# Raw weights loaded from the loop's second step on, and the first pair's queries loaded once and doubled by GpSimd

## The chip, the core and the metric

One core of a Trainium2 chip runs the whole program. The metric is the device time of one execution in microseconds; three runs of the kernel before have a median of 945.22 us. A core has five engines with queues of their own: TensorE (PE, matrix products and transposes; PEld is its weight load), VectorE (DVE), ScalarE (ACT), GpSimd (POOL) and SyncE (SP), which here only issues transfers. ScalarE and GpSimd can issue transfers too. Sixteen DMA engines move the data.

## What is computed

Attention over 4 batches of 8 heads (576 rows of 64), in which only scores within `tau` of the row's maximum count; then a two-dimensional Fourier transform whose real part is added, a norm, an MLP with two weight matrices, and a gated layer. All in float32.

```python
scores = scale * np.matmul(q, k.transpose(0, 1, 3, 2))
thresh = np.max(scores, axis=-1, keepdims=True) - tau
scores = np.where(scores >= thresh, scores, -1000000000.0)
attn = np.exp(scores - max); attn = attn / (sum + 1e-09); x = attn @ v
...
u = x + np.real(np.fft.fft(np.fft.fft(x, axis=1), axis=2))
un = (u - mu) / np.sqrt(var + 1e-06)
y = u + np.maximum(un @ w_ch1, 0.0) @ w_ch2
...
out = sigmoid(causal_conv(y, conv_w)) * (y @ w_val) @ w_out
```

## The kernel before

The program is written in the order in which each engine is to run it; no scheduler reorders anything. It has three stages: an attention loop that also does the Fourier transform and prepares the MLP's weights (to about 385 us), the MLP, and the gated layer.

**The loop.** Heads are taken in 16 pairs. A pair has nine tiles of 128 rows of scores, and one step `u` of the loop handles two tiles, so a pair lasts four and a half steps. In each step the atoms of the string `ORDER` are written out one after the other: for the step's two tiles the row maxima on VectorE (L571) and the threshold (L574, once in each step), the exponentials on ScalarE (L578), the masked product on VectorE (L588), and the next two tiles' scores on TensorE (L559). The tiles of the step before are normalised on GpSimd (L595), and those of two steps before are transposed on TensorE (L629). Between them `filler` puts matrix work from queues: the preparation of the next pair (`g_prep_qk`), the products with the values, and the Fourier transform.

**A pair's loads.** `load_qk(p, second)` brings the keys (`kn`, two loads of 128 KB, and a small one into `tn`), the last 64 query rows of both heads (`tn`, two small loads of the same rows), and the first 512 query rows (`qn`). Index `j` of `qn` is a copy: each head's queries are loaded twice from memory, for `j` = 0 and 1, so that a transpose gives the queries in both halves of the partitions. The keys go through SyncE's queue; for pair 0 `second` is ScalarE's queue, and for all later pairs it is SyncE's. The pool of these tiles has one buffer, so a pair's loads wait until the transposes of the pair before have read theirs. `g_prep_qk` then transposes on TensorE: keys (L244), last rows (L254), head 0's queries and head 1's (L263), with copies out of PSUM by VectorE (L250, L258) and ScalarE (L257, L265). For pair 0 this stands ahead of the loop, and the first scores need all of it.

**The raw weights.** The MLP's weights arrive as 64-bit words and are split into a high and a low part. They come in pieces of 512 KB; three raw buffers and two conversion rooms exist during the loop. `load_raw` issues a piece's load on GpSimd's queue whenever a raw buffer is free; `tick`, called at the end of each step, advances the clock (`clock[0]`) by one, hands on finished pieces and calls `load_raw`. The first such call is at the end of step 0, with the clock at 1, and it issues three loads. Nothing stands ahead of them on GpSimd's queue that waits for anything. A further call, `hooks["begin"]` at `u == 1`, finds no free buffer. A piece's conversion may begin when the clock is four (`LOAD`) past its load. It is a list of operations (L96 to L106 in `stages`): L96 and L97 on VectorE, L98 and L99 on ScalarE, L100, L101 and L102 on VectorE, and L106 on GpSimd, handed out by the atoms `WD`, `WA` and `WP`, a few in each step; so a piece in the loop visits VectorE in three steps. The first 18 pieces (`EARLY`) go back to memory (`e_h`, `e_l`, L921) and come again later; from the 19th on a piece needs a place that opens only behind the loop. Each piece's raw buffer is loaded anew at the end of the step in which it is finished, so the pieces follow one another at a fixed distance of three steps.

Of the kernel before, what the change touches and what calls it, by code (L numbers as in the profile page):

```python
# [21 lines left out]
B, H, S, D = 4, 8, 576, 64  # L22
# [4 lines left out]
MAIN, TAIL = 512, 64  # L27
# [37 lines left out]
@with_exitstack  # L65
def fused_kernel(ctx: ExitStack, tc: tile.TileContext, a: dict, out: bass.AP):
    dram = ctx.enter_context(tc.tile_pool(name="dram", bufs=1, space=DRAM))
    u_d = [dram.tile([DM, S], F32, name=f"u_d{b}") for b in range(B)]
    y_d = [dram.tile([DM, S], F32, name=f"y_d{b}") for b in range(B)]
    with tc.manual_schedule():  # L70
        wide = Wide(tc, ctx)
        conv_w = ConvW(tc, ctx, a, wide)
        fft = ctx.enter_context(ExitStack())
        with tc.tile_pool(name="ps_f", bufs=2, space=PSUM, side="right") as ps_f:
            hooks = {}
            attention = attention_fft(tc, fft, ps_f, a, u_d, dram, conv_w, hooks)
            mlp(tc, fft, ps_f, attention, hooks, a, u_d, y_d, dram, wide, conv_w.cw, out)
# [57 lines left out]
def attention_fft(tc, right, ps_f, a, u_d, dram, conv_w, hooks):  # L135
    nc = tc.nc
    PE, DVE, ACT, POOL, SP = nc.tensor, nc.vector, nc.scalar, nc.gpsimd, nc.sync
    left, right1 = ExitStack(), ExitStack()
    with ExitStack() as right2, ExitStack() as right2b, ExitStack() as right3, ExitStack() as right4, ExitStack() as scores, ExitStack() as turned:
# [39 lines left out]
        def load_qk(p, second=SP):  # L179
            b, hs = p // NP, slice(2 * (p % NP), 2 * (p % NP) + 2)  # L180
            kn = nat_p.tile([128, 2, 2, 2, D], F32, tag="kn", name="kn")
            qn = nat_p.tile([128, 2, 4, 2, D], F32, tag="qn", name="qn")
            tn = nat_p.tile([96, 2, 2, D], F32, tag="tn", name="tn")
            k, q = a["k"][b, hs].rearrange("h (g p) d -> p h g d", g=2), a["q"][b, hs]
            for j in range(2):
                SP.dma_start(out=kn[:, j], in_=k[j * 128:j * 128 + 128])
            SP.dma_start(out=tn[0:32], in_=k[256:HALF])
            for j in range(2):
                second.dma_start(out=tn[32:96, :, j], in_=q[:, MAIN:S].rearrange("h p d -> p h d"))
            for h in range(2):  # L190
                for j in range(2):
                    second.dma_start(out=qn[:, h, :, j], in_=q[h, 0:MAIN].rearrange("(t p) d -> p t d", p=128))
            nat[p] = tn, kn, qn

        def load_v(p):
# [37 lines left out]
        def g_prep_qk(p):  # L233
# [33 lines left out]
            if 0 < p < NPAIR - 1:  # L267
                load_qk(p + 1)
# [375 lines left out]
        LAG = 4  # L644
        SP.dma_start(out=ident, in_=a["ident"])
        load_qk(0, ACT)
        DVE.tensor_scalar(out=atau, in0=tau, scalar1=-1.0, scalar2=None, op0=ALU.mult)
        DVE.tensor_tensor(out=atau, in0=atau, in1=tau, op=ALU.max)
# [6 lines left out]
        while q_prep:  # L655
            fill(1e9)
            flush()
        load_qk(1)
        emit_s(0)
        emit_s(1)  # L660

        spare = 0.0
# [6 lines left out]
        for u in range(NT // 2 + 3):  # L669
            t = 2 * u  # L670
            on = [x for x in (t, t + 1) if x < NT]
            state["tile"] = t
            for x in on:
                p, h, i = tiles[x]
# [68 lines left out]
            for atom in ORDER.split():  # L743
                env[atom]()
            tq.clear()
            if u == 1:
                hooks["begin"]()
            hooks["tick"]()
            if left and NPAIR - 1 in kq:
                left.close()  # L750
# [33 lines left out]
def mlp(tc, right, ps_f, attention, hooks, a, u_d, y_d, dram, wide, cw, out):  # L784
    nc = tc.nc
    PE, DVE, ACT, POOL, SP = nc.tensor, nc.vector, nc.scalar, nc.gpsimd, nc.sync
    KB, FB = DM // 128, DFF // 128
# [5 lines left out]
    with ExitStack() as ctx, ExitStack() as top, ExitStack() as top2:  # L793
        def pool(name, bufs, stack=ctx, **kw):
            return stack.enter_context(tc.tile_pool(name=name, bufs=bufs, reuse_waits="tile", **kw))
# [3 lines left out]
        pieces = []  # L799
# [8 lines left out]
        heads = [0, 0]  # L808
        raws, spare = {}, {"raw": deque(), "cv": deque()}
        active, outbox, stored = deque(), [], deque()  # L810
        at, loaded, clock = [0], [0], [0]
# [42 lines left out]
        def more_room(kind, name):  # L854
            spare[kind].append((pool(name, 1), kind))
            load_raw()

        def load_raw():

            while spare["raw"] and loaded[0] < (len(pieces) if heads[1] == FB else 2 * FB):  # L860
                k = loaded[0]
                loaded[0] += 1
                src, _ = pieces[k]
                room = spare["raw"].popleft()
                room_pool, tag = room
                raws[k] = room, room_pool.tile([128, 512, 2], I32, tag=tag, name="raw", bufs=1), clock[0]
                d = raws[k][1].rearrange("p n t -> p (n t)")
                POOL.dma_start(out=d if len(src.shape) == 2 else d.rearrange("p (k f) -> p k f", k=KB), in_=src)
# [40 lines left out]
        def tick():  # L909

            clock[0] += 1
            while spent and spent[0][0] <= clock[0]:
                nxt[1] -= 1
                give(spent.popleft()[1])
            while stored and stored[0][0] <= clock[0]:
                spare["cv"].append(stored.popleft()[1])
            for k, room, dst in outbox:
                j, i = pieces[k][1]
                if isinstance(j, str) or k < EARLY:
                    for t, d in zip(dst, e_d[k] if k < EARLY else [d[i * 128:(i + 1) * 128] for d in w_d[j]]):  # L920
                        SP.dma_start(out=d, in_=f32(t))  # L921
                    written.add(k)
                    if k in wanted:
                        place(k)
                else:
                    placed.add(k)
                stored.append((clock[0] + (STORE if tail is None else 0), room))
                spare["raw"].append(raws.pop(k)[0])
            outbox.clear()
            load_raw()  # L930
# [233 lines left out]

        for kind in ("raw", "raw", "raw", "cv", "cv"):
            spare[kind].append((pool(f"mlp_{kind}{len(spare[kind])}", 1), kind))
        hooks["begin"] = load_raw

        norm, centred = None, True

# [362 lines left out]
```

## Time and profile before

| | us |
|---|---|
| median of 3 runs | 945.22 |
| lowest and highest run | 945.05, 945.52 |
| the profiled execution | 940.76 |
| its span | 939.0 |
| TensorE busy in it | 882.5 |
| VectorE busy | 561.6 |
| ScalarE busy | 453.0 |
| GpSimd busy | 365.0 |

The rows come from the one profiled execution, so times are placed on its span of 939.0 us, which starts at 0. A row of the timeline gives start, duration, engine, line, operation, output and input and count; what stands in brackets is the idle time of the engine ahead of it and what ended that. A queue that only issues transfers has a q behind its engine's name (SPq, ACTq). Line numbers are those of the kernel before.

### The profile page before, as it was taken

What the parts mean: (1) busy time and instruction counts of PE and PEld (TensorE: products, weight loads), DVE (VectorE), ACT (ScalarE), POOL (GpSimd) and SP (SyncE); (2) the same over time, 40 slices, a digit from 0 to 9 for tenths busy, and PEclk for the clock granted to TensorE, in tenths of its full rate; (3) what the DMA queues carried; (4) which work ended last, traced back from release to release, by engine and by line L of the source; (5) the groups of instructions that cost most, each with busy time, mean ns of one, the idle gap of its engine ahead of it and who ended that gap; (6) DMA issues with size and microseconds to landing.
All of it is one profiled execution on the core that took longest, in us unless ns stands there. A gap on an engine that the chain in (4) does not pass through costs nothing. (4 is left out here: it accounts for less than half of the span.)

```text
span 939.0 us, 14896 instructions
## 1 busy us (share of the span) xinstructions
PE 882.5 (94%) x5232; PEld 705.2 (75%) x5232; DVE 561.6 (60%) x1240; ACT 453.0 (48%) x915; POOL 365.0 (39%) x449
## 2 busy tenths in 40 slices
PE   3889899999999999899998999999999999999998
PEld 2555576656655675478876999999999989998897
DVE  4888888878887776415597243443412275735750
ACT  3777787777776766526355133213211313214432
POOL 1474654674457536613553421312111011037421
PEclk9999999999999999999998999999999999999999
DMA  7675545566555731496359523212120050233211
GB/s 173 164 191 130 165 115 163 159 195 152 168 149 166 186 96 61 145 351 211 106 194 359 213 90 123 86 45 84 45 73 1 1 170 11 90 129 118 74 46 68
DMA packets 136339, 123.61 MB, mean 132 GB/s; under 512 B 86742, under 2 KB 100294, under 8 KB 136264
## 3 DMA queue, kind: packets, MB, share of 16 engines
q1 hardware_dynamic: 126760, 97.57, 33.9%
q0 software_dynamic: 6960, 24.49, 8.5%
q10 hardware_dynamic: 2544, 0.59, 0.4%
q8 instruction: 42, 0.69, 0.3%
q14 instruction: 33, 0.27, 0.1%
HBM read 90.11 MB, written 37.22 MB: 136 GB/s over the span
## 5 line engine op out<-in xcount | busy, mean ns | idle before, releaser
L1060 DVE SCALAR_TENSOR_TENSOR hl<-h,hh 128x448 fp32r<-128x448 f32 (+1 forms) x80 | 51.0, 637 | 204.1 <-ACT hh L1059 204.1
L1059 ACT ACTIVATE hh<-h 128x448 fp32r<-128x448 f32 (+1 forms) x80 | 44.5, 556 | 256.6 <-PE h L1056 256.6
L595 POOL TENSOR_SCALAR p<-p,su 128x576 f32<-128x576 f32 x144 | 108.8, 762 | 90.3 <-DVE su L685 74.1
L588 DVE SCALAR_TENSOR_TENSOR p<-s,thr,e 128x576 f32<-128x576 f32 x144 | 112.4, 815 | 32.2 <-ACT e L578 14.4
L559 PE MATMUL s<-kt,qt 64*128 64x288 f32 (+1 forms) x640 | 99.6, 441 | 27.1 <-DVE p L588 27.1
L1072 PE MATMUL c<-hl,w1h 128*128 128x448 f32 (+1 forms) x320 | 118.9, 371 | 0.7 <-DVE hl L1060 0.7
L1072 PE MATMUL c<-hh,w1h 128*128 128x448 f32 (+1 forms) x320 | 119.0, 372 | 0.0
L1072 PE MATMUL c<-hh,w1l 128*128 128x448 f32 (+1 forms) x320 | 118.8, 371 | 0.0
L578 ACT ACTIVATE e<-s,neg 128x576 f32<-128x576 f32 x144 | 99.4, 737 | 26.1 <-DVE neg L571 25.8
L571 DVE TENSOR_REDUCE neg<-s 128x1 f32<-128x576 f32 x144 | 101.4, 745 | 14.8 <-PE s L559 14.6
L559 PEld LDWEIGHTS s<-kt,qt 64*128 64x128 f32 (+1 forms) x640 | 45.2, 175 | 69.0 <-issue 27.8
L638 ACT ACTIVATE m<-t 128x512 f32<-128x512 f32 x144 | 84.6, 588 | 6.8 <-PE t L629 6.8
L1056 PE MATMUL h<-unh,w0l 128*128 128x448 f32 (+1 forms) x320 | 81.3, 376 | 3.9 <-POOL w0l L106 3.8
L1056 PE MATMUL h<-unh,w0h 128*128 128x448 f32 (+1 forms) x320 | 81.0, 375 | 3.0 <-ACT w0h L105 2.2
L304 PE MATMUL f<-m,v 128*64 128x320 f32 (+1 forms) x512 | 81.9, 422 | 1.5 <-ACT m L638 1.2
L629 PE MATMUL t<-ident,p 128*128 128x128 f32 x576 | 77.7, 277 | 3.4 <-POOL xf L334 1.9
L1056 PE MATMUL h<-unl,w0h 128*128 128x448 f32 (+1 forms) x320 | 80.7, 374 | 0.0
L629 PEld LDWEIGHTS t<-ident,p 128*128 128x128 f32 x576 | 63.6, 140 | 19.2 <-issue 9.3
L1056 PEld LDWEIGHTS h<-unh,w0l 128*128 128x128 f32 x320 | 60.3, 189 | 12.6 <-POOL w0l L106 5.4
L1056 PEld LDWEIGHTS h<-unh,w0h 128*128 128x128 f32 x320 | 60.1, 189 | 11.4 <-ACT w0h L105 3.0
L106 POOL TENSOR_TENSOR ct<-raw 128x512 fp32r<-128x512 f32 x26 | 28.8, 1113 | 99.5 <-DVE raw L102 55.0
L1072 PEld LDWEIGHTS c<-hl,w1h 128*128 128x128 f32 x320 | 60.1, 188 | 8.0 <-DVE hl L1060 1.1
(218 smaller groups left out, 1575.4 us busy)
## 6 DMA issues: line engine op xcount, KB each, us to landing
raw<-in_moe_w_ch POOLq DMA_DIRECT2D x32, 512.0 KB, 5.5
qn<-in_q SPq DMA_DIRECT2D x60, 128.0 KB, 3.5
xs<-xt SPq DMA_DIRECT2D x16, 288.0 KB, 3.6
e_h<-cx SPq DMA_DIRECT2D x18, 256.0 KB, 3.8
e_l<-ct SPq DMA_DIRECT2D x18, 256.0 KB, 5.8
w0h<-e_h SPq DMA_DIRECT2D x18, 256.0 KB, 16.1
w0l<-e_l SPq DMA_DIRECT2D x18, 256.0 KB
w1h<-e_h SPq DMA_DIRECT2D x18, 256.0 KB, 5.5
```

What stands on the lines that cost most here:

```text
L304: PE.matmul(out=f[h * 64:h * 64 + 64, 0:n], lhsT=w, rhs=r, start=(t == 0), stop=(t == 4))
L559: PE.matmul(out=s[o, c, 0:HALF], lhsT=qt[w, hh, q], rhs=kt[w, hh, :], start=True, stop=True)
L571: DVE.tensor_reduce(out=neg[i][:, j, 0:1], in_=sc[g][:, :, 0:HALF], axis=AX.XY, op=ALU.max, negate=True)
L578: ACT.activation(e, sc[g][:, :, 0:HALF], AF.Exp, bias=neg[g // 2][:, g % 2, 0:1], scale=1.0)
L588: DVE.scalar_tensor_tensor(out=p_view(g).rearrange("p (a b) -> p a b", a=2), in0=sc.pop(g)[:, :, 0:HALF], scalar=thr[g // 2][:, j], in1=ex ...
L595: POOL.tensor_scalar(out=v, in0=v, scalar1=su, scalar2=1.0, op0=ALU.mult, op1=ALU.mult)
L629: PE.matmul(out=f[:, t, :], lhsT=pv[:, t * 128:(t + 1) * 128], rhs=ident, is_transpose=True, start=(t == 0), stop=(t == 3))
L638: tq.append(lambda: ACT.activation(o, fv, AF.Copy))
L1056: PE.matmul(out=f[:, 0:n], lhsT=ww[:, k * 128:(k + 1) * 128], rhs=x[:, k, 0:n], start=(i == 0), stop=(i == 3 * KB - 1))
L1059: ACT.activation(hh, f[:, 0:n], AF.Relu)
L1060: DVE.scalar_tensor_tensor(out=hl, in0=f[:, 0:n], scalar=0.0, in1=f32(hh), op0=ALU.max, op1=ALU.subtract)
L1072: PE.matmul(out=ch[c][o][:, 0:n], lhsT=ww[:, o * 128:(o + 1) * 128], rhs=x, start=(at_ == 0 and i == 0), stop=(at_ == FB - 1 and i == 2))
```

## The change

`load_raw` loads nothing while the clock is 1 or less, so the first three raw loads are issued at the end of step 1 in place of step 0. The call `hooks["begin"]` is gone. For pair 0 alone (the branch in which `second` is not SyncE) each head's queries are loaded once, into `j` = 0, and GpSimd copies them to `j` = 1; the order of ScalarE's loads is now head 0's queries, the two loads of last rows, head 1's queries. For the other pairs the loads stay as they were.

```diff
@@ load_qk
-            for j in range(2):
-                second.dma_start(out=tn[32:96, :, j], in_=q[:, MAIN:S].rearrange("h p d -> p h d"))
-            for h in range(2):
+
+            def queries(h, j):
+                second.dma_start(out=qn[:, h, :, j], in_=q[h, 0:MAIN].rearrange("(t p) d -> p t d", p=128))
+
+            def last_queries():
                 for j in range(2):
-                    second.dma_start(out=qn[:, h, :, j], in_=q[h, 0:MAIN].rearrange("(t p) d -> p t d", p=128))
+                    second.dma_start(out=tn[32:96, :, j], in_=q[:, MAIN:S].rearrange("h p d -> p h d"))
+
+            if second is SP:
+                last_queries()
+                for h in range(2):
+                    for j in range(2):
+                        queries(h, j)
+            else:
+                for h in range(2):
+                    queries(h, 0)
+                    if h == 0:
+                        last_queries()
+                    POOL.tensor_copy(qn[:, h, :, 1], qn[:, h, :, 0])
             nat[p] = tn, kn, qn
@@ attention loop
-            if u == 1:
-                hooks["begin"]()
             hooks["tick"]()
@@ load_raw
-            while spare["raw"] and loaded[0] < (len(pieces) if heads[1] == FB else 2 * FB):
+            while clock[0] > 1 and spare["raw"] and loaded[0] < (len(pieces) if heads[1] == FB else 2 * FB):
@@ mlp
-        hooks["begin"] = load_raw
```

What this moves, at three places. Lines of the changed kernel are other numbers: its L609 is the normalisation L595, its L880 the raw load L868.

GpSimd's queue from the program's start on, before:

```order
L1529 UNCONDITIONAL_BRANCH
L868 DMA raw<-in_moe_w_ch 128x4x256
L868 DMA raw<-in_moe_w_ch 128x1024
L868 DMA raw<-in_moe_w_ch 128x4x256
L595 ISA
L595 TENSOR_SCALAR p<-p,su 128x576 x2
L206 DMA cdh<-in_cdh 128x1032
```

and now (its L206 COPY is the new copy of the queries, its L220 the load of the constants):

```order
L1540 UNCONDITIONAL_BRANCH
L206 COPY qn<-qn 128x4x64 x2
L609 ISA
L609 TENSOR_SCALAR p<-p,su 128x576 x2
L880 DMA raw<-in_moe_w_ch 128x4x256
L880 DMA raw<-in_moe_w_ch 128x1024
L880 DMA raw<-in_moe_w_ch 128x4x256
L220 DMA cdh<-in_cdh 128x1032
```

The three raw loads went from ahead of step 1's two normalisations to behind them, and the two copies stand first.

ScalarE's queue at the start, with the semaphores that a row waits for (`tn` are the last rows, `qn` the queries of one head), before:

```order
L165 DMA tau_sb<-in_tau 128x1
L167 ACT_TABLE_LOAD
L167 ACTIVATE atau<-alpha 128x1 [waits DVE_49]
L189 DMA tn<-in_q 64x2x64 x2
L192 DMA qn<-in_q 128x4x64
L192 DMA qn<-in_q 128x4x64 [waits DMAHW0_49]
L192 DMA qn<-in_q 128x4x64 [waits DMAHW2_49]
L192 DMA qn<-in_q 128x4x64 [waits DMAHW4_49]
```

and now:

```order
L165 DMA tau_sb<-in_tau 128x1
L167 ACT_TABLE_LOAD
L167 ACTIVATE atau<-alpha 128x1 [waits DVE_49]
L190 DMA qn<-in_q 128x4x64
L194 DMA tn<-in_q 64x2x64 x2
L190 DMA qn<-in_q 128x4x64 [waits DMAHW0_49]
```

Two loads are gone, head 0's queries moved ahead of the last rows, and head 1's, the last, wait for the semaphore for which the second query load waited before.

VectorE in two steps of the loop, the first of which has the keys' copies of a new pair (L250 and L258; now L264 and L272), before; L588 are the masked products (now L602), L685 the reciprocal that opens a step (now L699):

```order
L588 SCALAR_TENSOR_TENSOR p,su<-s,thr,e 128x576 x2
L250 COPY kt<-f 128x2x256
L258 COPY kt<-f 128x2x32
L101 SCALAR_TENSOR_TENSOR raw<-raw,ct 128x512
L102 TENSOR_SCALAR raw<-cx 128x512
L96 TENSOR_SCALAR cx<-raw 128x512
L685 RECIPROCAL su<-su 128x2
L571 TENSOR_REDUCE neg_193<-s 128x1 x2
L574 TENSOR_REDUCE thr<-neg_193 128x2
L588 SCALAR_TENSOR_TENSOR p,su<-s,thr,e 128x576 x2
L97 TENSOR_SCALAR ct<-raw 128x512
L685 RECIPROCAL su<-su 128x2
```

and now:

```order
L602 SCALAR_TENSOR_TENSOR p,su<-s,thr,e 128x576 x2
L264 COPY kt<-f 128x2x256
L272 COPY kt<-f 128x2x32
L100 SCALAR_TENSOR_TENSOR cx<-raw,cx 128x512
L699 RECIPROCAL su<-su 128x2
L585 TENSOR_REDUCE neg_193<-s 128x1 x2
L588 TENSOR_REDUCE thr<-neg_193 128x2
L602 SCALAR_TENSOR_TENSOR p,su<-s,thr,e 128x576 x2
L101 SCALAR_TENSOR_TENSOR raw<-raw,ct 128x512
L102 TENSOR_SCALAR raw<-cx 128x512
L96 TENSOR_SCALAR cx<-raw 128x512
L699 RECIPROCAL su<-su 128x2
```

The three operations L101, L102 and L96 moved from the step with the keys' copies into the next. The same shift by one step runs through the whole loop on VectorE, ScalarE and GpSimd (steps with the keys' copies and these three together: five before, none now), and SyncE's stores of the finished pieces move with it. TensorE's order is the same in every row, and behind the loop every engine's order is the same.

## Rows read from the trace of the kernel before

**Rows 1.** Busy time by stretch; columns: stretch, length, busy of each engine, clock, DMA.

```profile
core 0: us, PE busy (x) PEld busy (x) DVE busy (x) ACT busy (x) POOL busy (x), PEclk, DMA share, GB/s
...
512.00:707.00 195.00, 195.00 (x955) 178.83 (x954) 72.10 (x127) 48.70 (x87) 44.50 (x43) 1.00 0.29 100
```

**Rows 2.** Timeline of the first 16 us; start, duration, engine, line, operation.

```profile
1.20 0.96 SPq L186 DMA_DIRECT2D kn<-in_k  x2
1.26 2.26 POOL L868 DMA_DIRECT2D raw<-in_moe_w_ch  x3 [0.81 <-POOLq L1522]
...
10.50 0.90 PE L244 MATMUL f<-ident,kn 128*128 128x128 f32 x3 [5.25 <-DMA kn<-in_k]
...
13.21 0.71 PEld L263 LDWEIGHTS f<-ident,qn 128*128 128x128 f32 x4 [0.23 <-issue]
```

**Rows 3.** Timeline, ScalarE's queue at 3.8 us: the second query load.

```profile
3.87 0.64 ACTq L192 DMA_DIRECT2D qn<-in_q  x1
```

**Rows 4.** Busy time by stretch, as in rows 1.

```profile
6.00:8.00 2.00, 0.00 (x0) 0.00 (x0) 0.00 (x0) 0.00 (x0) 0.00 (x0) 1.00 1.06 350
...
16.00:32.00 16.00, 10.21 (x71) 6.17 (x72) 13.60 (x35) 10.23 (x20) 5.89 (x9) 1.00 0.80 188
```

**Rows 5.** DMA issues of the whole run; count, size of each, median us to landing.

```profile
qn<-in_q SPq DMA_DIRECT2D x60, 128.0 KB, 3.5
...
kn<-in_k SPq DMA_DIRECT2D x32, 128.0 KB, 3.2
```

**Rows 6.** DMA issues from 14 to 23 us: a value load behind queries.

```profile
v<-in_v SPq DMA_DIRECT2D x1, 128.0 KB, 5.4
```

**Rows 7.** Groups on GpSimd by shape: count, busy us, mean ns, idle before.

```profile
L595 POOL TENSOR_SCALAR p<-p,su 128x576 f32<-128x576 f32 x144 | 108.8, 762 | 90.3 <-DVE su L685 74.1 <-PE f L263 10.0 <-PE s L559 4.0
...
L334 POOL COPY xf<-xt 128x2 f32<-128x2 f32 x16 | 3.1, 193 | 1.0
```

**Rows 8.** Timeline of 19 to 29 us, GpSimd and its reader.

```profile
19.73 1.47 POOL L595 TENSOR_SCALAR p<-p,su 128x576 f32<-128x576 f32 x2 [16.22 <-DVE su L685]
...
21.16 0.59 POOL L206 DMA_DIRECT2D cdh<-in_cdh  x1
...
24.39 1.46 POOL L595 TENSOR_SCALAR p<-p,su 128x576 f32<-128x576 f32 x2 [2.64 <-DVE su L685]
...
28.29 0.87 PE L629 MATMUL t<-ident,p 128*128 128x128 f32 x6
```

**Rows 9.** Line 868 from 30 to 385 us; durations in ns, min/median/max.

```profile
L868 POOL DMA_DIRECT2D raw<-in_moe_w_ch x18: 582/728/872, 55.9 to 318.8; - x18
```

**Rows 10.** Groups on VectorE from 20 to 385 us: the conversion's operations.

```profile
L97 DVE TENSOR_SCALAR ct<-raw 128x512 int32<-128x512 int32 x18 | 16.6, 921 | 0.0
L100 DVE SCALAR_TENSOR_TENSOR cx<-raw,cx 128x512 int32<-128x512 int32 x18 | 13.3, 738 | 0.0
L101 DVE SCALAR_TENSOR_TENSOR raw<-raw,ct 128x512 f32<-128x512 uint32 x18 | 13.1, 728 | 0.0
...
L96 DVE TENSOR_SCALAR cx<-raw 128x512 int32<-128x512 int32 x18 | 7.8, 432 | 0.0
L102 DVE TENSOR_SCALAR raw<-cx 128x512 int32<-128x512 int32 x18 | 7.6, 421 | 0.0
```

**Rows 11.** Busy time of two single steps, then of eight steps twice.

```profile
119.57:124.86 5.29, 4.71 (x37) 3.50 (x37) 5.12 (x13) 4.77 (x11) 2.47 (x4) 1.00 0.04 13
124.86:128.73 3.87, 3.87 (x32) 2.25 (x29) 3.73 (x9) 3.45 (x9) 3.84 (x6) 1.00 0.92 262
...
221.17:262.52 41.35, 39.18 (x300) 28.80 (x297) 34.62 (x86) 29.98 (x66) 21.38 (x30) 1.00 0.57 151
318.77:360.48 41.71, 39.55 (x302) 29.23 (x302) 29.99 (x76) 27.43 (x61) 22.35 (x29) 1.00 0.39 103
```

**Rows 12.** Busy time of one step with conversions, and the same one batch later.

```profile
246.91:251.93 5.02, 3.97 (x29) 2.49 (x27) 4.39 (x12) 3.65 (x10) 1.61 (x3) 1.00 0.82 193
344.11:348.87 4.76, 3.71 (x28) 2.23 (x27) 3.21 (x9) 3.69 (x9) 1.97 (x4) 1.00 0.75 236
```

**Rows 13.** Timeline at 270 us, VectorE: the longest of line 97.

```profile
270.32 4.11 DVE L97 TENSOR_SCALAR ct<-raw 128x512 int32<-128x512 int32 x1
```

## The prediction

> **What bounds the kernel now.** I read three views: the busy time by stretch, the timeline of the first 16 us, and the busy time step by step through the attention loop. Behind the attention, TensorE has no gap at all: 195.00 us busy in a stretch of 195.00 us [rows 1]. In the loop it is close to that: 39.18 of 41.35 us over eight steps [rows 11]. So a gain must either shorten the start, where TensorE does nothing, or take idle time out of the loop.
>
> The start is one wait. The first pair's keys come in two loads issued from 1.20 us on (0.96 us for both, so the second from 1.68 us), yet the transposes that need the second go on only at 10.50 us, released by that load [rows 2]. That is 8.8 us for 128 KB. Over the whole run a key load lands 3.2 us after its issue and a query load after 3.5 us [rows 5]. What is different here is the company: GpSimd issues three raw-weight loads of 512 KB at 1.26 us [rows 2], and between 6 and 8 us the DMA engines are full (share 1.06, 350 GB/s) while every compute engine shows 0.00 us of work [rows 4]. From 10.50 us on, a fixed chain runs to the first scores; the transposes of the second head's queries in it start at 13.21 us [rows 2]. All later work hangs on that chain through the steps, so whatever the start loses the whole run loses.
>
> **The change, part by part. (a) The raw loads leave the start.** The keys then see an ordinary landing: 1.68 + 3.2 = 4.9 us, and the key chain starts 10.50 - 4.9 = 5.6 us earlier.
>
> **(b) The queries of the first pair.** ScalarE's DMA queue issues four loads in place of six. The last one, head 1's queries, still waits for the semaphore for which the second query load waited before, and that was issued at 3.87 us [rows 3]. I let it go at 3.87 us again: landing 3.87 + 3.5 = 7.4 us. Then the new GpSimd copy, 256 columns. No such copy is in the trace; a copy of 2 columns takes 193 ns and a one-input operation of 576 columns 762 ns [rows 7], so about 1 ns per column, and 193 + 254 = 0.45 us by interpolation, which I take because the two ends are alike in kind; the bounds are 0.19 and 0.76 us. Ready at 7.8 us, against a use at 13.21 us: a head start of 5.4 us. This is 0.2 us less than the key chain's, so the queries are last now, narrowly. Head 0's copy is earlier in every part (its load is the first in the queue, and it is copied first), and the two last-query loads stay ahead of head 1's load in the queue: neither is last. Head start: **5.4 us**. Bounds: with a landing of 5.4 us, the slow row for a load of this size [rows 6], and a copy of 0.76 us, the queries are ready at 10.0 us and 3.2 us are won; however fast they are, the keys set 5.6 us. A loss is excluded here: less is moved, and nothing is put ahead of the keys.
>
> **(c) Where the raw loads go.** They now stand on GpSimd behind step 1's two normalisations, which ran from 19.73 us for 1.47 us [rows 8]: shifted by 5.4, until 15.8 us. Three issues cost 3 x 0.73 = 2.2 us, at worst 3 x 0.87 = 2.6 us [rows 9], and the constants' load behind them 0.59 us [rows 8]. GpSimd is free for step 2's normalisations at 18.6 to 19.0 us; they became ready at 24.39 - 5.4 = 19.0 us. Their reader, the transposes seen at 28.29 us [rows 8], wants them at 22.9 us, so with 1.47 us of work there are 2.4 us of cover. Cost: nothing; were the cover gone, each further us would go to the path. Their traffic, 1.5 MB, falls into a stretch in which the DMA engines were 0.80 busy [rows 4], so loads in it land later. Those are loads for the third pair, for values and for constants, used several steps on, and the raw weights themselves are read four steps after their load by the code: about 15 us at 3.87 us a step [rows 11], against a slow landing of 5.4 us [rows 6]. I cost this at nothing.
>
> The trace shows GpSimd's issues of such loads in the midst of VectorE's work at no more than 0.87 us [rows 9]. The Trainium skill, "SBUF — State Buffer", section "A bandwidth-pool intuition that's wrong (but worth ruling out)", speaks against this move: GpSimd writes its DMA descriptors through a port that VectorE's two-port operations lock, and a load of 620 ns alone took some 3100 ns beside such a copy. By that figure the three issues would cost 9.3 us and end the cover; by the row they cost 2.2 us and the sum is as above.
>
> **(d) The conversions start one step later.** This is the term I know least. Each raw piece is split by VectorE in three visits: L97 in one step, L100 in the next, then L101, L102 and L96 (0.73 + 0.42 + 0.43 = 1.58 us [rows 10]). TensorE's order of work is unchanged, but every visit from the start to the 18th piece moves by one step against the keys' copies and the FFT's work. Of each nine steps three get the heavy visit. Two kinds change.
> - Before, the heavy visit fell on steps with the keys' copies: from 119.57 us, 5.29 us with VectorE busy 5.12 and TensorE 4.71; the next step, with L97 alone, took 3.87 us, VectorE 3.73 [rows 11]. After: the first has L100 in place of the heavy visit, VectorE 5.12 - 1.58 + 0.74 = 4.28, so TensorE bounds it at 4.71; the next gets the heavy visit in place of L97. That one's mean is 0.92 us, and undisturbed it would take the 0.42 us of L102, the same kind of operation [rows 10]; with the middle, 0.67 us, VectorE has 3.73 - 0.67 + 1.58 = 4.64 us, and with the 0.17 us in which it was not busy in the step before, 4.81. Together 9.52 against 9.16: +0.36 us, five times in the loop: +1.8 us.
> - The heavy visit leaves a step that VectorE's chain bounds: 5.02 us with it, 4.76 us for the same step later on, when no conversions are left [rows 12]. That is 0.26 us won, five times: -1.3 us.
>
> In the other steps TensorE is the bound either way: eight steps with conversions took 41.35 us, the same eight without took 41.71 us [rows 11]. So the term is **+0.5 us**, with 0 and +1.8 us as its near ends, since the two kinds may balance or the gain may stay out.
>
> **Sum.** -5.4 + 0.5 = -4.9 us. The profiled execution took 940.76 us (span 939.0 and 1.8 us around it); the median of the runs shown, 945.22 us, is 4.5 us longer than that one, and I hang the difference on the median: **940.3 us** (for a profile like that one: 935.9 us, span 934.1). A measurement of this kernel can tell about 0.2%, 1.9 us, from no change.
>
> **Rivals.**
> 1. *The new phase of the conversions pays.* For: the five steps with the keys' copies had 5.29 - 4.71 = 0.58 us of idle TensorE each. Against: the next step gets what they lose. If only the -1.3 us holds: 945.2 - 5.4 - 1.3 = 938.5 us.
> 2. *Slower: VectorE and GpSimd lock each other out in the new phase.* At 270.32 us one L97 took 4.11 us [rows 13]; the mean of 18 is 0.92 us against L102's 0.42, so these stalls already add 18 x 0.5 = 9.0 us to VectorE [rows 10]. Moved by a step, other visits (L102 and L96 are of the same kind as L97) meet GpSimd's runs. If the stalls double and each falls on the path: 945.2 - 5.4 + 9.0 = 948.8 us. It decides the sign from 5.4 us, or 0.3 us per piece. Against: in the eight steps above, stalls included, conversions cost TensorE nothing. The Trainium skill, the same page, section "Who interferes with whom", names the mechanism: copies and scalar operations on VectorE can take the port pair that is GpSimd's only one, and whoever comes second waits for the whole instruction. By that rule the trace agrees that GpSimd's unbroken runs make L97 wait.
> 3. *Slower: the raw loads' issues hold GpSimd.* If each of the three issues waits as long as the longest stall seen, 4.11 us [rows 13], GpSimd is free at 15.8 + 12.3 + 0.6 = 28.7 us, its normalised rows are ready at 30.2 us where 22.9 us is wanted, and 7.3 us go: 945.2 - 4.9 + 7.3 = 947.6 us. Against: 18 issues without one above 0.87 us [rows 9]. This is what the rule of the Trainium skill told in (c) would do here.
> 4. *The queries' new path eats the head start.* Landing 5.4 us, copy 0.76 us, and the unrelieved +1.8 us of (d): 945.2 - 3.2 + 1.8 = 943.8 us.
> 5. *The change doesn't do what it says:* the keys were not held by the raw loads but by the queries' small rows. Then only 256 KB less at 350 GB/s count, 0.7 us, and with (d) the time is 945.2 - 0.7 + 0.5 = 945.0 us. Against: the 3.2 us that key loads take elsewhere with the same queries behind them.
>
> **How the numbers follow.** Forecast 0.62; rival 1 0.16; rival 2 0.05; rival 3 0.03; rival 4 0.09; rival 5 0.05. The predicted time is 940.3 us. The forecast's own spread is 939.6 us (5.6 won, nothing paid) to 942.6 us (4.4 won, the middle of its bounds, and 1.8 paid). With rivals 1 and 4 in it the range is 938.0 to 944.3 us and leaves out 0.13. Faster by over 0.2%: 0.62 + 0.16 = 0.78. Within 0.2%: rivals 4 and 5, 0.14. Slower: rivals 2 and 3, 0.08.
>
> **What would show it.** (a) The keys' second part of the transposes starts near 5 us, not 10.5. (b) The second head's query transposes start near 7.8 us and are released by GpSimd's copy, which shows 0.4 to 0.5 us. (c) Three raw issues right behind step 1's normalisations, none above 0.9 us, and no wait of TensorE on GpSimd in step 3. (d) The first step's threshold comes about 5.4 us earlier, and at the end of the attention about 4.9 us are left: each us less is the conversions' new phase. The prediction is wrong if the first scores come less than 4.5 us earlier, or if the lead shrinks or grows by more than 1.8 us between 20 and 385 us.

## The result and the profile after

The kernel before took 945.16 us (median of 4 runs), the changed kernel 937.38 us (935.33 to 938.12, 4 runs): a ratio of 0.9916, 95% interval 0.9901 to 0.9931, which is 7.8 us less (6.5 to 9.4). Forecast were 940.3 us with a range from 938.0 us: the direction is right, the gain is 2.9 us larger than forecast and the time 0.6 us below the range. The profiled execution of the changed kernel took 937.77 us, its span is 936.0 us. From L193 to L745 the changed kernel's line numbers are 14 higher (L574, the threshold that I use to mark a step, is L588); from L868 to L1084 they are 12 higher.

The start, timeline of the changed kernel (start, duration, engine, line; as rows 2 and 3):

```profile
3.90 0.38 ACTq L190 DMA_DIRECT2D qn<-in_q  x1
...
5.69 0.90 PE L258 MATMUL f<-ident,kn 128*128 128x128 f32 x3 [0.64 <-DMA kn<-in_k]
...
6.58 0.40 POOL L206 COPY qn<-qn 128x256 f32<-128x256 f32 x1 [1.06 <-DMA qn<-in_q]
...
6.63 0.69 DVE L264 COPY kt<-f 128x512 f32<-128x512 f32 x1 [1.38 <-PE f L258]
...
7.42 1.94 PE L277 MATMUL f<-ident,qn 128*128 128x128 f32 x8 [0.39 <-POOL qn L206]
...
9.29 2.29 PE L573 MATMUL s<-kt,qt 64*128 64x288 f32 x8
...
12.43 0.16 DVE L588 TENSOR_REDUCE thr<-neg 128x2 f32<-128x4 f32 x1
...
15.16 1.47 POOL L609 TENSOR_SCALAR p<-p,su 128x576 f32<-128x576 f32 x2 [8.18 <-DVE su L699]
...
16.58 2.28 POOL L880 DMA_DIRECT2D raw<-in_moe_w_ch  x3
...
21.06 1.46 POOL L609 TENSOR_SCALAR p<-p,su 128x576 f32<-128x576 f32 x2 [1.68 <-DVE su L699]
```

The transposes that had waited for the keys until 10.50 us [rows 2] go on at 5.69 us. The copy of head 1's queries takes 0.40 us and ends at 6.98 us. The row at 7.42 us holds the transposes of both heads; the first four are head 0's, and head 1's start at 8.30 us (13.25 us before, just behind the weight load at 13.21 us in [rows 2]). The row names GpSimd's copy as what was waited for, but both copies had ended by 6.98 us; what ended last ahead of 7.42 us is VectorE's copy of the keys, 6.63 + 0.69 = 7.32 us. The first threshold comes at 12.43 us. In the kernel before, the query transposes and the threshold stand here:

```profile
12.30 2.03 PE L263 MATMUL f<-ident,qn 128*128 128x128 f32 x8
...
17.00 0.16 DVE L574 TENSOR_REDUCE thr<-neg 128x2 f32<-128x4 f32 x1
```

So the head start is 4.6 us. The three raw issues take 2.28 us together (0.98, 0.55 and 0.76 us) and stand where step 1's normalisations end, as the prediction placed them.

The conversions of the loop, grouped (answering rows 10; count, busy us, mean ns):

```profile
L100 DVE SCALAR_TENSOR_TENSOR cx<-raw,cx 128x512 int32<-128x512 int32 x18 | 13.3, 739 | 0.0
L101 DVE SCALAR_TENSOR_TENSOR raw<-raw,ct 128x512 f32<-128x512 uint32 x18 | 12.7, 705 | 0.0
L97 DVE TENSOR_SCALAR ct<-raw 128x512 int32<-128x512 int32 x18 | 11.9, 661 | 0.0
L96 DVE TENSOR_SCALAR cx<-raw 128x512 int32<-128x512 int32 x18 | 8.8, 491 | 0.0
L102 DVE TENSOR_SCALAR raw<-cx 128x512 int32<-128x512 int32 x18 | 8.1, 447 | 0.0
```

The same work, but L97 takes 11.9 us in place of 16.6: its long stalls have become short ones. The two steps of rows 11 now read so (columns as there):

```profile
116.59:121.21 4.62, 4.04 (x33) 3.09 (x32) 4.45 (x12) 4.61 (x12) 3.03 (x5) 1.00 0.36 81
121.21:126.17 4.96, 4.96 (x41) 3.08 (x39) 4.39 (x11) 3.73 (x9) 2.32 (x4) 1.00 0.50 112
```

5.29 and 3.87 us before, that is 9.16 us together; 4.62 and 4.96 us now, 9.58 us.

### The profile page after: what moved, and what is told of

It is laid out like the page before. It is cut to its first block, busy times and chain, and to the rows that moved or that the text cites. A ratio compares the mean times of both kernels' runs of the same rounds, so it can differ in the third digit from the quotient of the medians.

```text
span 936.0 us, 14888 instructions
## 1 busy us (share of the span) xinstructions
PE 884.3 (94%) x5232; PEld 708.0 (76%) x5232; DVE 553.5 (59%) x1240; ACT 451.2 (48%) x915; POOL 368.0 (39%) x451
## 5 line engine op out<-in xcount | busy, mean ns | idle before, releaser
L609 POOL TENSOR_SCALAR p<-p,su 128x576 f32<-128x576 f32 x144 | 109.9, 769 | 91.1 <-DVE su L699 71.5
L602 DVE SCALAR_TENSOR_TENSOR p<-s,thr,e 128x576 f32<-128x576 f32 x144 | 112.6, 815 | 39.8 <-ACT e L592 21.9
L1084 PE MATMUL c<-hl,w1h 128*128 128x448 f32 (+1 forms) x320 | 118.9, 371 | 0.5 <-DVE hl L1072 0.5
L1084 PE MATMUL c<-hh,w1h 128*128 128x448 f32 (+1 forms) x320 | 118.8, 371 | 0.0
L1084 PE MATMUL c<-hh,w1l 128*128 128x448 f32 (+1 forms) x320 | 118.7, 371 | 0.0
L1068 PEld LDWEIGHTS h<-unl,w0h 128*128 128x128 f32 x320 | 61.2, 191 | 7.2
L1084 PEld LDWEIGHTS c<-hl,w1h 128*128 128x128 f32 x320 | 60.1, 188 | 7.7 <-DVE hl L1072 0.9
```

Source lines behind the costliest of these rows:

```text
L602: DVE.scalar_tensor_tensor(out=p_view(g).rearrange("p (a b) -> p a b", a=2), in0=sc.pop(g)[:, :, 0:HALF], scalar=thr[g // 2][:, j], in1=ex ...
L609: POOL.tensor_scalar(out=v, in0=v, scalar1=su, scalar2=1.0, op0=ALU.mult, op1=ALU.mult)
L1068: PE.matmul(out=f[:, 0:n], lhsT=ww[:, k * 128:(k + 1) * 128], rhs=x[:, k, 0:n], start=(i == 0), stop=(i == 3 * KB - 1))
L1084: PE.matmul(out=ch[c][o][:, 0:n], lhsT=ww[:, o * 128:(o + 1) * 128], rhs=x, start=(at_ == 0 and i == 0), stop=(at_ == FB - 1 and i == 2))
```

## The experiments

A step k ends with the k-th threshold (L574), so its length is the difference of two starts of that line; 72 of them make the loop. Each test is given with its median and its ratio to the kernel before on the same chip, with the 95% interval.

**Both kernels again** (no edit).

> The kernel before, unchanged. The change took 7.8 us off the median (945.16 to 937.38) but the two profiled executions differ by 3.0 us only (940.76 and 937.77), because the profiled execution of the kernel before was 4.4 us faster than its own four timed runs. Theory A (that one profile was an exceptional execution): this kernel's profile lands near 945 us here, and its rows show where the 4 us lie. Theory B (the chip or the pairing makes the difference): it lands near 941 us beside runs of the same, and the true gain is about 3 to 4 us.

> The changed kernel, unchanged. Theory A: 937 to 938 us against 945 us on the same chip, 7 to 8 us less. Theory B: about 937 us against 941 us, 3 to 4 us less. In both, the second head's query transposes start between 7.4 and 8.4 us.

Measured: 944.64 us for the kernel before (0.9998, 0.9982 to 1.0014; 12 runs between 941.80 and 947.02) and 937.19 us for the changed one (0.9920, 0.9905 to 0.9936; 6 runs between 936.09 and 939.53). The result stands, and the runs of the kernel before lie further apart.

**Each part alone.** The raw loads alone (e3): queries as before, and only

```
-            while spare["raw"] and loaded[0] < ...
+            while clock[0] > 1 and spare["raw"] and loaded[0] < ...
```

The queries alone (e4): the changed kernel without this condition.

> Only the raw loads' delay; the first pair's queries are loaded twice as before. If the raw loads held the keys, the keys' transposes go on at about 5.7 us as in the changed kernel, but the fourth query load waits for a semaphore of an earlier load and lands near 9.5 us: head start about 3.5 us in place of 4.6, time about 1 us above the changed kernel's. If the fewer query loads were what helped, the keys' transposes go on near 10 us and the time is that of the kernel before.

> Only the queries' new path; the raw loads are still issued in the loop's first step, but stand behind the two copies on GpSimd's queue, so they go out near 7 us, after the first pair's loads have landed. The conversions keep their old phase. If the head start is the whole gain, this has all of it (the changed kernel's time within 1 us). If the later phase of the conversions in the loop gives back 3 us, as the step times of the two profiles suggest around 275 us, this one is about 3 us above the changed kernel.

Measured: e3 936.79 us (0.9913, 0.9894 to 0.9931), e4 944.06 us (0.9999, 0.9984 to 1.0014). The delay of the raw loads is the whole gain, the queries' new path none of it; e3 is not 1 us slower than the changed kernel, as expected, but as fast. The new path even holds the keys up a little. In e3 the keys' transposes go on at 5.14 us, behind this weight load:

```profile
5.13 0.51 PEld L244 LDWEIGHTS f<-ident,kn 128*128 128x128 f32 x3 [0.43 <-DMA kn<-in_k]
```

In all five kernels with late raw loads and the queries as before (e3, e6, e7, e12, e13) they go on between 5.14 and 5.22 us, in the three executions with the new path (the changed kernel, e2, e4) between 5.68 and 5.73 us. Head 0's queries, 128 KB, are now issued at 1.45 us, between the keys' two loads, where small loads of 32 KB stood.

In e4 the raw loads are only pushed behind GpSimd's copies. Its timeline:

```profile
6.93 2.26 POOL L880 DMA_DIRECT2D raw<-in_moe_w_ch  x3
...
12.46 0.16 DVE L588 TENSOR_REDUCE thr<-neg 128x2 f32<-128x4 f32 x1
...
16.74 0.55 PE L268 MATMUL f<-ident,tn 96*128 96x96 f32 x2 [3.71 <-DMA tn<-in_q]
```

The first pair is as early as in the changed kernel. Then the raw loads, issued at 6.93 us, hold up the second pair's small loads as they had held up the first pair's: TensorE waits 3.71 us for the last queries, step 2 takes 7.90 us in place of 3.98, and the head start is spent. What counts is when the raw loads go out and which small loads they meet, not only that the first pair's loads are ahead of them.

**Start and phase apart.** e5 leaves the raw loads at the start and takes the pieces up one step later. e6 sends the loads late and takes the pieces up in the old steps. e7 sends them late and takes the pieces up two steps later. In the record of a piece (against the kernel before for e5, against e3 for e6 and e7):

```
e5:  raws[k] = room, ..., max(clock[0], 2)
e6:  raws[k] = room, ..., clock[0] - (k < 3)
e7:  raws[k] = room, ..., clock[0] + (k < 3)
```

> Only the conversions move: the three raw loads go out at the start as in the kernel before, but their pieces are taken up one step later, so that VectorE, ScalarE, TensorE and SyncE carry the same instructions in the same order as in e3. Theory 'two shares' (the start is worth 4.2 to 4.8 us, the conversions' phase about 3): first threshold at 16.6 to 17.0 us as before, no L97 above 3 us in steps 34 and 52, each of these 5.4 to 5.7 us long, time 941.0 to 942.5 us. Theory 'start alone' (the phase costs 0.5 us as predicted, or nothing; the rest of the gain is what early loads hold up in the first steps): 944 to 945.5 us.

> Only the loads move: the three raw loads go out on GpSimd after step 1 as in e3, but the pieces are taken up in the same steps as in the kernel before; every engine except GpSimd has the order of the kernel before. Theory 'two shares': first scores near 9 us, first threshold 11.8 to 12.5 us, steps 34 and 52 either 5.3 or 7.3 us as in the kernel before (an L97 of 4 us where it is 7.3), time 939.5 to 941.5 us. Theory 'start alone': 936.5 to 938 us.

> The loads as in e3, the conversions two steps later than in the kernel before instead of one. Theory 'two shares', in its form 'the old phase is the bad one' (the two stalls of L97 belong to it): steps 34 and 52 near 5.5 us, time within 1.5 us of e3, 935.5 to 938.5 us. In its form 'the new phase is the good one': 939 to 941 us, as with the start alone. Theory 'start alone': as e3, 936.8 us, with steps 34 and 52 as they fall.

| kernel | first threshold | step 34 | step 52 | 72nd threshold | span | median |
|---|---|---|---|---|---|---|
| before, first profile | 17.00 | 5.34 | 7.28 | 385.49 | 939.0 | 945.16 |
| e5, phase alone | 17.76 | 5.55 | 5.54 | 385.99 | 939.9 | 942.86 |
| e6, start alone | 11.98 | 7.27 | 7.28 | 382.13 | 937.1 | 937.78 |
| e3, both | 11.81 | 5.54 | 5.53 | 379.18 | 933.3 | 936.79 |
| e7, two steps later | 12.27 | 5.47 | 5.47 | 385.73 | 940.7 | 942.88 |
| after | 12.43 | 5.54 | 5.54 | 381.66 | 936.0 | 937.38 |

The ratios are 0.9986 (0.9969 to 1.0003) for e5, 0.9930 (0.9906 to 0.9955) for e6 and 0.9985 (0.9965 to 1.0005) for e7. The expectation for the phase falls in size: e5 gained 1.2 us, not 3, and its interval includes no change at all. The start alone gave 6.2 us by the medians (4.2 to 8.9 by the interval), more than the theory of two shares said and as the theory of the start alone had it. What held is the pattern of steps 34 and 52: both at 7.3 us in e6, both at 5.5 us in e5 and e3. And e7, which came out as none of its theories said, shows that a later phase is not better in general. Its two steps are short too, but it lost 6.1 us against e3 by the medians, and 6.6 us at the 72nd threshold. Of these, 2.2 us are a later first threshold and slow steps 2 and 3 (see the last section). Another 1.5 us are step 60 (6.91 us against 5.39), where TensorE waits for a pair's small loads, beside which a raw load was issued (in e3 the raw load goes out at 316.76 us, behind them):

```profile
309.60 0.59 POOL L868 DMA_DIRECT2D raw<-in_moe_w_ch  x1 [0.30 <-POOL ct L106]
...
315.09 0.36 PE L254 MATMUL f<-ident,tn 96*128 96x96 f32 x2 [1.41 <-DMA tn<-in_q]
```

So the phase of the conversions also sets when the next raw loads go out, and which small loads they meet. The rest of e7's loss is spread over other steps, and no run here separates it.

**Is a microsecond at the start worth one at the end?** The first half of the first keys is loaded twice (e8) or three times (e9) in e3, each load waiting for the one before; here the line numbers are one higher.

```
+                for _ in range(2 if p == 0 and j == 0 else 1):
                     SP.dma_start(out=kn[:, j], in_=k[j * 128:j * 128 + 128])
```

> e3 with the first half of the first pair's keys loaded twice, each load waiting for the one before it; no raw load is near. The start comes later by x, read from the first threshold against 11.8 us in e3 (an estimate: 2 to 3.2 us, a landing). Theory 'one for one': time 936.8 + x. Theory 'a late start costs more than itself' (which would explain why the start alone gave 6.2 us where the first threshold came 4.7 us earlier): 936.8 + 1.3 x or more. Theory 'something later swallows it': 936.8 + 0.7 x or less.

> As e8, the first half of the keys loaded three times, so that the start comes later by about twice as much, 4 to 6.4 us (estimate), as late as in the kernel before or a little later. 'One for one': 936.8 + x, 941 to 943 us. 'Costs more than itself': 943 to 945 us, as the kernel before with its raw loads at the start. 'Swallowed': 941 us or less.

Measured: first threshold at 15.42 us (3.6 us later than in e3), 939.13 us (0.9954, 0.9935 to 0.9973), so 2.3 us lost by the medians; and at 17.57 us (5.8 us later), 942.34 us (0.9982, 0.9966 to 0.9998), so 5.5 us lost. By the theories' own bounds the smaller step is "swallowed" and the larger "one for one". But e3 ran on another chip, the runs of e8 and e9 lie up to 6.9 us apart, and by the ratios the losses are about 3.9 and 6.5 us. The traces say more still: at the 72nd threshold e8 is 5.9 us and e9 8.0 us behind e3, in the spans 5.3 and 7.3 us, because step 3 (5.18 and 5.28 us against 4.65) and step 13 (6.77 us in both against 5.10) are longer than in e3. So the medians speak against "costs more than itself", the traces lean towards it, and it stays open what a microsecond at the start is worth.

**What varies in the kernel before?** Two more executions with a trace.

> The kernel before once more, for a third execution with a trace. Theory 'two stalls by chance': steps 34 and 52 are each 5.3 or 7.3 us, step 12 is 3.9 or 4.5 us, steps 3 and 4 are 4.65 and 3.62 or up to 1.4 us longer together, and the time follows the sum: 940.8 us with one stall and quick early steps, 943.9 us with two stalls and slow ones. Rival 'the time varies elsewhere': the table of steps is as in the first execution and the time is not.

> A fourth execution of the kernel before, with the same two readings as e10: the time follows the stalls in steps 34 and 52 and the early steps, or it varies elsewhere.

| execution of the kernel before | first threshold | steps 3 and 4 | step 34 | step 52 | 72nd threshold | span |
|---|---|---|---|---|---|---|
| first profile | 17.00 | 8.27 | 5.34 | 7.28 | 385.49 | 939.0 |
| e1 | 16.63 | 9.59 | 7.27 | 7.28 | 388.90 | 942.1 |
| e10 | 16.99 | 8.27 | 7.28 | 7.28 | 387.00 | 942.2 |
| e11 | 17.13 | 8.26 | 7.28 | 7.28 | 387.22 | 942.7 |

Three of four executions, and e6 as well, have the long stall in both steps. The profile of before, on which the prediction was built, has it in one; so does e4, which has the old phase too (7.29 and 5.34 us). The time does not follow the sum of the steps alone: e1 is 1.9 us behind e10 at the 72nd threshold, and their spans are the same within 0.1 us. This is the stall, from the timeline of e10:

```profile
173.22 0.82 DVE L588 SCALAR_TENSOR_TENSOR p<-s,thr,e 128x576 f32<-128x576 f32 x1
173.38 0.74 POOL L595 TENSOR_SCALAR p<-p,su 128x576 f32<-128x576 f32 x1
...
173.95 4.11 DVE L97 TENSOR_SCALAR ct<-raw 128x512 int32<-128x512 int32 x1
174.10 0.79 POOL L448 TENSOR_TENSOR xr<-xr,sm 128x289 f32<-128x289 f32 x1
174.85 0.79 POOL L341 TENSOR_TENSOR xel<-xf,xeh 128x289 fp32r<-128x289 f32 x1
175.63 0.73 POOL L595 TENSOR_SCALAR p<-p,su 128x576 f32<-128x576 f32 x1
176.34 0.68 POOL L450 TENSOR_TENSOR xr<-xr,dd 128x287 f32<-128x287 f32 x1
...
176.99 0.79 POOL L341 TENSOR_TENSOR xol<-xf,xoh 128x287 fp32r<-128x287 f32 x1
177.98 0.15 DVE L685 RECIPROCAL su<-su 128x2 f32<-128x2 f32 x1
178.06 1.40 DVE L571 TENSOR_REDUCE neg<-s 128x1 f32<-128x576 f32 x2
```

L97, 0.42 us of work, becomes ready while GpSimd runs L595, and ends only when GpSimd's unbroken run has ended at 177.78 us. The next maxima (L571) stand behind it on VectorE, and the step grows by 1.9 us. L588 just before runs beside GpSimd in its usual 0.82 us. The same place in the changed kernel:

```profile
172.05 0.42 DVE L102 TENSOR_SCALAR raw<-cx 128x512 int32<-128x512 int32 x1
172.39 0.42 DVE L96 TENSOR_SCALAR cx<-raw 128x512 int32<-128x512 int32 x1
172.55 1.15 POOL L106 TENSOR_TENSOR ct<-raw 128x512 fp32r<-128x512 f32 x1 [2.05 <-DVE raw L102]
...
174.23 0.16 DVE L588 TENSOR_REDUCE thr<-neg 128x2 f32<-128x4 f32 x1
...
175.97 1.82 DVE L97 TENSOR_SCALAR ct<-raw 128x512 int32<-128x512 int32 x1
176.05 1.46 POOL L609 TENSOR_SCALAR p<-p,su 128x576 f32<-128x576 f32 x2
```

The heavy visit now stands in this step, and it meets an idle GpSimd: GpSimd has waited 2.05 us for L102. L97 comes a step later and meets a run of 1.46 us: 1.82 us in place of 4.11 (as rows 13).

**Is it the form of L97?** In the loop, L97 is written as an operation with two inputs, like L100, in the old phase (e12, from e6) and in the new one (e13, from e3).

```
-("D", lambda: V.tensor_scalar(out=t, in0=high, scalar1=0x1FF, scalar2=None, op0=ALU.bitwise_and)),
+("D", lambda: V.scalar_tensor_tensor(out=t, in0=high, scalar=0x1FF, in1=high,
+                                     op0=ALU.bitwise_and, op1=ALU.bitwise_and) ...),
```

> e6 (raw loads after step 1, conversions in the steps of the kernel before) with one instruction of each conversion in the loop written in another form: L97, until now a TENSOR_SCALAR with one input, becomes a SCALAR_TENSOR_TENSOR with the same input twice (the form of L100 and L101, which take 0.65 to 0.75 us and of which none was above 1.5 us). Same values, same place in VectorE's order. Theory 'the form is what waits': L97 takes 0.65 to 0.75 us in every step, also in steps 34 and 52 where it took 4.11; these are 5.3 to 5.7 us long in place of 7.27; time of e6 less 3 to 3.9 us, 933.9 to 935.2 us. Rival 'VectorE waits for GpSimd in any form there': 7.27 us remain, 937.5 to 938.5 us.

> The same form of L97 in e3 (raw loads after step 1, conversions one step later), where L97 took at most 1.8 us in this part of the loop. Theory 'the form is what waits': at most 1 us is won, 935.8 to 937 us, so that e12 without its stalls is as fast as this one or faster, because apart from the two stalls the later phase costs about 0.8 us (steps of e3 against those of e6 without steps 34 and 52). Rival: the later phase is better of itself, e13 under e12 by 1 us or more.

Measured: e12 938.90 us (0.9948, 0.9926 to 0.9969), e13 937.83 us (0.9926, 0.9902 to 0.9951). The theory of the form falls. In e12, at the old place:

```profile
170.18 4.37 DVE L97 SCALAR_TENSOR_TENSOR ct<-raw 128x512 int32<-128x512 int32 x1
```

Steps 34 and 52 take 7.54 and 7.56 us. Where nothing holds it up L97 takes 0.69 us instead of 0.42, and by the medians (from different chips) both kernels are 1.0 to 1.1 us slower than e6 and e3. The place in GpSimd's work decides, not the choice between these two forms. Whether some third form escapes was not tried. The Trainium skill, "SBUF — State Buffer", section "Who interferes with whom", counts both forms among those that can meet GpSimd: copies and scalar operations in the mode that uses two ports, and operations with two inputs in SBUF. By that the trace agrees, 4.11 us for the one form and 4.37 us for the other; the scores that L588 reads are in PSUM, and it runs undisturbed.

## Why the prediction was wrong, step by step

**(a) The raw loads leave the start: right, but 0.8 us too much.** The keys' transposes go on at 5.69 us where 4.9 was forecast and 10.50 stood before [rows 2]. Rival 5 is refuted by e3 and e4: with the queries as before and only the raw loads moved the whole gain is there, with only the queries moved none of it.

**(b) The queries: the times right, the order wrong.** The second query load issues at 3.90 us (3.87 forecast), the copy takes 0.40 us (0.45), and head 1's queries are ready at 6.98 us (7.8). But they are not last, as the prediction had it: the keys are, whose copy by VectorE ends at 7.32 us. That nothing is put ahead of the keys was wrong too: head 0's queries are issued between the two key loads, and the keys' transposes go on 0.5 us later than with the old path. The head start is 4.8 us at the keys' transposes, 5.0 us at the first scores (14.26 to 9.29 us) and, because the first eight score matmuls take 2.29 us in place of 1.71, 4.6 us at the first threshold; forecast were 5.4. e3 starts earlier with six loads on ScalarE's queue (11.81 us). Rival 4 is refuted.

**(c) The raw issues behind step 1: right.** They take 0.98, 0.55 and 0.76 us (0.97, 0.55 and 0.76 us at the start of the kernel before), none is held for long, so rival 3 is refuted, though the first is above the 0.9 us that the prediction set. No raw issue of the changed kernel's loop stood beside L96, L97 or L102, so what such a meeting would cost is not shown; the second pair of normalisations starts at 21.06 us when its input is ready.

**(d) The conversions' phase: wrong, and this is the step that failed.** It forecast +0.5 us. Its first kind was read from one pair of steps, 24 and 25 (rows 11), and taken five times. The five pairs are 15 and 16, 24 and 25, 33 and 34, 42 and 43, 51 and 52. In the changed kernel against e10 three of them came out at +0.2 to +0.4 us (+0.36 forecast). In the other two the second step is one of the stalls: steps 34 and 52 fall from 7.28 to 5.54 us, and the two pairs lose 2.4 us each. The second kind came out as forecast or a little better: 5.02 to 4.61 us for the step of rows 12, -0.41 us (-0.26 forecast). Without steps 34 and 52 the loop of e3 takes 0.7 us more than that of e6: 367.37 - 11.07 = 356.30 us against 370.15 - 14.55 = 355.60 us. Included in this are steps 35 and 53, where L97 now stands, each 1.0 to 1.1 us longer. The two stalls together give -3.5 us, so by these two traces the term is about -2.8 us.

The stall was on record [rows 13], and rival 2 asked whether such stalls might double; that the move might end them was not priced. Against rival 2 stood the sentence that in eight steps, "stalls included", conversions cost TensorE nothing; but the eight steps, from 221.17 to 262.52 us, hold no L97 above 0.75 us, and the long ones at 174.03 and 270.32 us lie outside. Rival 2 did not come: L97 fell from 16.6 to 11.9 us.

**The median.** The prediction hung the 4.5 us between its profiled execution and the median on as a constant. It is none: the executions e1, e10 and e11 are 3.1 to 3.7 us longer than the first profile. The second stall makes step 34 longer by 1.9 us, of which 1.5 us are left at the 72nd threshold (e10), and the change removes it too. Against the first profile the stalls are worth 1.5 us, against the common execution 3.5 us.

**The sum as measured**, changed kernel against e10, at the 72nd threshold: head start 16.99 - 12.43 = 4.56; steps 34 and 52, 3.48; the other steps of the new phase -0.7; and slow steps 2 and 3 of the changed kernel (4.35 and 6.05 us against 3.98 and 4.66) -1.76. That gives 5.6 us; the trace has 387.00 - 381.66 = 5.34 us. That this is near the 4.9 us forecast is luck: a head start that was put too high and slow steps that the sum did not have nearly cancel a phase with the wrong sign. Against the first profile, on which the forecast was built, only 385.49 - 381.66 = 3.83 us are left there, and the spans differ by 3.0 us. Against e10 the spans differ by 6.2 us (6.7 against e11, 6.1 against e1). The second profile of the changed kernel, e2, is 1.7 us longer than the first, so traced pairs without the first profile lie between 4.4 and 6.7 us, and the medians 7.3 to 7.8 us apart. The rest, 0.6 to 3.4 us, is not explained, and so neither is all of the 2.9 us by which the forecast missed the median: behind the loop the traced executions differ by up to 3 us (553.2 to 556.2 us from the 72nd threshold to the end) without any tie to the change that I found.

One thing stays in conflict. Step by step the phase is worth 2.8 us; by the medians of e5, of e6 against e3 and of e12 against e13 it is worth 1.0 to 1.2 us, with intervals of more than 1.5 us to either side. The traced run of e6 is the slowest of its six and that of e3 the second fastest of its six, so this pair of traces may show more than the usual difference; how often the untraced runs had the stalls, no run shows. In e5, 0.95 us goes in step 28, where L96 waits for a store:

```profile
145.05 0.78 DVE L96 TENSOR_SCALAR cx<-raw 128x512 int32<-128x512 int32 x1 [0.68 <-DMA e_h<-cx]
```

What the runs show clearly is the head start's part, and that the long stall stands in at least one of steps 34 and 52 in every traced execution of the old phase (both in five of seven) and in none of the new phase (seven). That the forecast +0.5 us had the wrong sign follows from these traces; the timed runs point the same way, but their intervals do not settle it. Rival 1 named the right direction, for another reason.

## What to carry to other kernels

One profile is one draw. Before hanging a difference between the profile and the median on a constant, look in the profile for a wait that could strike more often than it did there, and price its end as well as its doubling. Before one place is multiplied by five, look at all five. When a change shifts side work by a step, go through the steps in which that work already stalls, not only through those in which it fits: its neighbours on the other engine decide. And bulk loads near the start should go behind the small loads of every early step, not only of the first.

## What was not expected of the hardware

L97 waited through GpSimd's whole unbroken run, five instructions after the one beside which it became ready, with no gap between any two in the record; it was let in at none of these seams. The stall is not certain. In the first profile it took 4.11 us at 270.32 us [rows 13], but at 174.03 us, with the same work around it, 2.17 us. There the record fits its being let in at the third seam, ahead of an L595 that took 1.01 us in place of 0.73:

```profile
174.03 2.17 DVE L97 TENSOR_SCALAR ct<-raw 128x512 int32<-128x512 int32 x1
...
175.71 1.01 POOL L595 TENSOR_SCALAR p<-p,su 128x576 f32<-128x576 f32 x1
```

TensorE was slow in the first steps of some executions. The changed kernel (first row) and e3 (second row), windows from 20 us on (columns as in rows 1):

```profile
20.00:24.00 4.00, 3.90 (x16) 2.33 (x16) 3.19 (x9) 2.05 (x4) 1.46 (x2) 0.57 1.10 342
```

```profile
20.00:24.00 4.00, 2.91 (x22) 1.91 (x21) 3.59 (x9) 2.96 (x6) 1.85 (x3) 1.00 1.08 327
```

The granted clock is 0.57 there in the one, near the lower of the two levels (1.2 and 2.4 GHz), and 1.00 in the other. In the four microseconds before, TensorE was busy for 1.56 us in the one and 1.93 us in the other. But eight score matmuls took 2.29 us in the changed kernel already at 9.29 and 13.66 us, where the record has 1.00, against 1.90 and 1.49 us in e3 at 8.97 and 13.04 us. Steps 2 to 4 cost 1.8 us more than in e3 in three traced executions (the changed kernel, e2, e7), 1.3 us in e1, which starts late, and 0.4 to 0.6 us in four others; what decides it stays open.
